# An adaLN attention block on one Trainium2 core: the opening of the kernel reordered (third x tile later, one copy on GpSimd, K rows and shift in another order)

## The chip, the core and the metric

The kernel runs on one core of a Trainium2 chip. Five engines work in it side by side, each through its own instruction queue in order: TensorE (PE in the profile; PEld is its weight load), VectorE (DVE), ScalarE (ACT), GpSimd (POOL) and SyncE (SP), which here only issues transfers from HBM to the on-chip memory (SBUF) and back. TensorE writes into the accumulation memory (PSUM), which VectorE and ScalarE read. The metric is the device time of one execution in microseconds (us), lower is better.

## What is computed

Inputs are bfloat16: x (2, 256, 1152), c (2, 1152), wqkv (1152, 3456), wo (1152, 1152), w_mod (1152, 6912).

```python
mod = (silu(c) @ w_mod).reshape(B, 6, 1, D)
shift_a, scale_a, gate_a, ... = mod[:, 0], mod[:, 1], mod[:, 2], ...
h = layernorm(x) * (1 + scale_a) + shift_a
q, k, v = split(h @ wqkv)                      # no bias, one head of width D
p = softmax(einsum("bqd,bkd->bqk", q, k) * D ** -0.5)
a = einsum("bqk,bkd->bqd", p, v) @ wo
out = x + gate_a * a                           # shift_m, scale_m, gate_m are not used
```

## The kernel before

**Tiles.** The 512 tokens are four tiles t = 0 to 3 of 128 (tiles 0 and 1 are batch 0, tiles 2 and 3 batch 1); the width D = 1152 is nine blocks k of 128. Everything is fed to TensorE with features on the partitions, so x is centred, turned by TensorE (`turned`, tiles `tp…`), and kept as `xnT[k, token]`.

**The order is written out.** The wrappers `vec`, `sca`, `ten`, `spq`, `gps` record every instruction, and `pin` (line 91) makes each engine run its list in the order of the program text. An engine that waits therefore holds up everything behind it. Because all instructions pass through the wrapper, the profile gives them all line 78; they are told apart by the names of their tiles.

**The opening (to about 31 us).** While the weights stream in, K is computed ahead of Q and V, in an unusual way: scale and centring are applied at once, `hTs = xnT * (1 + scale)`; the 1/sigma of a key is left for the softmax (a factor on the scores, from `rstd_bc`), and what shift adds to K is the same for every key, so softmax drops it. K needs `hTs` only. Q and V need `hT = xnT * rstd * (1 + scale) + shift`, hence the shift.

- *Transfers* (lines 151 to 174, in this order on SP): x tiles 1, 0, 3; the first three blocks of the scale weights `wS` in five pieces (`PAIRS`); K weights `wK` row 0 in two pieces, row 1; x tile 2; row 2; then scale weights and K rows in turns, the shift weights `wH`, the rest.
- *Fillers* (line 185): 13 products of no use, which keep TensorE running until data is there.
- *silu(c)*: VectorE makes `scT_f` (line 191); a ScalarE copy, `silu_rep` (line 201), repeats it 27 times into `scT_rep`, the moving operand of the scale products.
- *Scale, first part* (`scale_A`, line 307): 27 products into `psS0` and `psSA`, four rows of them behind the turned tile 1, five behind the turned tile 0.
- *Means*: tile 1 from VectorE's statistics, tiles 0 and 3 by ScalarE (`act_mean`, two instructions), tile 2 half by ScalarE and half by VectorE. `centre` (VectorE) writes `xc`.
- *K*: six accumulators `accs` (NACC = 6 blocks of 128 output features) take `k_part` (one block k, some of the tokens) as `hTs` becomes ready, later `k_step` (one block k, all 512 tokens). Output blocks 6 and 7 are held in two halves: k = 0 to 2 in `psE`/`early` (`early_half`), and k = 3 to 8 "parked" in `parked` (`k_block`). Output block 8 is `last_k`, nine products.
- *Scale, second and third part*: `psM` (blocks 3 to 5) and `psL` (blocks 6 to 8), each 27 products, then VectorE's `scaled_part`: one add and six `scaled` (one per block and batch).
- *Variance*: `dve_stats` (VectorE), `act_var` (ScalarE), then a GpSimd chain `rstd_parts`, TensorE's `rstd_turn` and `rstd_spread`, ScalarE's copy to `rstd_bc`, and nine VectorE products `xnT *= rstd_bc`.
- *Shift* (`shift_rows`, 36 products into `psH`), VectorE's block transpose to `sh`, then 18 instructions `modulated` that make `hT`: piece i is block i // 2 of batch i % 2; where i % 3 == 2 ScalarE makes it, else VectorE.

In the text of the program, the order around the shift is: `k_step(8)`; parked 6 and 7 (12 products); `psH`; the nine products of `last_k`; then Q, whose first product needs both pieces of `hT[0]`.

**The rest.** Q (81 products of 512 columns), scores `s_ps`, V, attention times V, the output product; VectorE sums the gate (`gacc`) meanwhile and GpSimd adds it over the partitions (`gate_bc`). PSUM: six buffers "mm", one "pa", one "pb"; a tile waits until its buffer's last reader is done.

Of the kernel before, what the change touches and what calls it, by code (L numbers as in the profile page):

```python
# [7 lines left out]
ACT = mybir.ActivationFunctionType  # L8
# [8 lines left out]
def kernel(  # L17
# [82 lines left out]
    def tok(b):  # L100
        return slice(b * N, (b + 1) * N)
# [40 lines left out]
    def load_x(t):  # L142
        spq.dma_start(out=x_sb[:, t, :], in_=x_f[t * P : (t + 1) * P, :])

    def load_mod(tile_, which, k0, k1, c0, c1):
        spq.dma_start(out=tile_[:, k0:k1, c0:c1], in_=wmod_v[:, k0:k1, which, c0:c1])

    def load_k(k0, k1, c0=0, c1=D):
        spq.dma_start(out=wK[:, k0:k1, c0:c1], in_=wqkv_v[:, k0:k1, D + c0 : D + c1])
# [2 lines left out]
    CA = KA * P  # L152
    load_x(1)
    load_x(0)
    load_x(3)
    for k0, k1 in PAIRS:
        load_mod(wS, 1, k0, k1, 0, CA)
    load_k(0, 1, 0, CA)
    load_k(0, 1, CA, WE)
    load_k(1, 2, 0, WE)  # L160
# [19 lines left out]
    def fillers(n):  # L180
        for _ in range(n):
            ten.matmul(junk_ps, lhsT=junk_rhs, rhs=junk_rhs.unsqueeze(1).to_broadcast([P, 4, P]),
                       start=True, stop=True)

    fillers(13)
    e_sb = small.tile([P, 2 * KT], F32, tag="e_sb")
    sca.activation(out=e_sb, in_=cT, func=ACT.Exp, scale=-1.0)
    scT_f = const.tile([P, KT, B], F32)
# [10 lines left out]
        )  # L199

    def silu_rep():
        sca.copy(out=scT_rep, in_=scT_f.unsqueeze(2).to_broadcast([P, KT, NR // B, B]))

    def sc_rhs(kk):
        return scT_rep[:, kk].rearrange("p r b -> p (r b)")
# [18 lines left out]
    def var_eps(t):  # L224
        gps.tensor_scalar(out=rstd[:, t : t + 1], in0=mv[:, t, 1:2], scalar1=1.0, scalar2=EPS,
                                op0=ALU.mult, op1=ALU.add)

    def act_mean(t):
        sca.activation(out=xc[:, t, :], in_=x_sb[:, t, :], func=ACT.Copy, accum_out=sums[:, t, 0:1])
        sca.activation(out=mv[:, t, 0:1], in_=sums[:, t, 0:1], func=ACT.Copy, scale=1.0 / D)  # L230

    HALF = D // 2
    half_sum = const.tile([P, 1], F32)

    def act_half_mean(t):
        sca.activation(out=xc[:, t, 0:HALF], in_=x_sb[:, t, 0:HALF], func=ACT.Copy, accum_out=sums[:, t, 0:1])

    def dve_half_mean(t):
        vec.reduce_sum(out=half_sum, in_=x_sb[:, t, HALF:], axis=AX.X)
        vec.tensor_scalar(out=mv[:, t, 0:1], in0=half_sum, scalar1=sums[:, t, 0:1], scalar2=1.0 / D,  # L240
                          op0=ALU.add, op1=ALU.mult)

    def act_var(t):
        sca.activation(out=square, in_=xc[:, t, :], func=ACT.Square, accum_out=sums[:, t, 1:2])
        gps.tensor_scalar(out=rstd[:, t : t + 1], in0=sums[:, t, 1:2], scalar1=1.0 / D, scalar2=EPS,
                                op0=ALU.mult, op1=ALU.add)
# [5 lines left out]
    def turned(tp, cols):  # L252
        for j, (t, k) in enumerate(cols):
            ten.transpose(tp[:, j, :], xc[:, t, k * P : (k + 1) * P], ident)

    def tiles_of(t, k0, k1):
        return [(t, k) for k in range(k0, k1)]

    def from_psum(eng, t, k0, k1, tp, j0=0):
        dst, srct = xnT[:, k0:k1, t * P : (t + 1) * P], tp[:, j0 : j0 + k1 - k0, :]  # L260
        if eng is vec:
            vec.tensor_copy(out=dst, in_=srct)
        else:
            sca.copy(out=dst, in_=srct)
# [22 lines left out]
    def rstd_spread():  # L287
# [9 lines left out]
    qkT = act.tile([P, 2 * KT, T], BF16)  # L297
    early = const.tile([P, NEARLY, T], F32)

    psSA = psum_a.tile([P, KA - 1, NR], F32, tag="pa")  # L300
    ten.matmul(psSA.rearrange("p j r -> p (j r)"), lhsT=ones_bf[0:1, :],
               rhs=ones_row[0:1, 0 : (KA - 1) * NR], start=True, stop=False, skip_group_check=True)
    psS0 = psum_b.tile([P, NR], F32, tag="pb")
    ten.matmul(psS0, lhsT=ones_bf[0:1, :], rhs=ones_row[0:1, 0:NR], start=True, stop=False,
               skip_group_check=True)

    def scale_A(kk):
        for j in range(KA):
            ten.matmul(
                psS0 if j == 0 else psSA[:, j - 1, :], lhsT=wS[:, kk, j * P : (j + 1) * P], rhs=sc_rhs(kk),  # L310
                start=False, stop=(kk == KT - 1), skip_group_check=True,
            )

# [24 lines left out]
    def one(t):  # L338
        return slice(t * P, (t + 1) * P)

    def scaled(k, sl, scalar):
        vec.tensor_scalar(out=hTs[:, k, sl], in0=xnT[:, k, sl], scalar1=scalar, scalar2=None, op0=ALU.mult)
# [40 lines left out]
    act_mean(0)  # L383
    centre(0)
    silu_rep()
    act_mean(3)

    def bank(name="tp", n=KT - KA, pool=psum, tag="mm"):
        return pool.tile([P, n, P], BF16, tag=tag, name=name)

    tp1a, tp1b, tp0a, tp0b = bank(n=KA), bank(), bank(n=KA), bank()
    turned(tp1a, tiles_of(1, 0, KA))
    turned(tp1b, tiles_of(1, KA, KT))
    from_psum(vec, 1, 0, KA, tp1a)
    from_psum(vec, 1, KA, KT, tp1b)
    for kk in range(4):
        scale_A(kk)
    turned(tp0a, tiles_of(0, 0, KA))
    turned(tp0b, tiles_of(0, KA, KT))
    from_psum(vec, 0, 0, KA, tp0a)  # L400
    from_psum(sca, 0, KA, KT, tp0b)
    for kk in range(4, KT):
        scale_A(kk)
    act_var(0)

    accs = [psum.tile([P, T], F32, tag="mm", name="acc") for _ in range(NACC)]
    scaled(0, tok(0), psS0[:, 0:1])
    vec.tensor_copy(out=s1p[:, 1:KA, :], in_=psSA[:, :, 0:B])
    vec.tensor_copy(out=s1p[:, 0, :], in_=psS0[:, 0:B])
    scaled(1, tok(0), s1p[:, 1, 0:1])  # L410
    centre(3)
    for k in range(2, KA):
        scaled(k, tok(0), s1p[:, k, 0:1])
    dve_stats(3, 0)
    psE = psum_a.tile([P, NEARLY, N], F32, tag="pa")
    k_part(0, tok(0), first=True)
    early_half(0, 0, psE)
    tp3 = bank(n=KT - 1, pool=psum_b, tag="pb")
    turned(tp3, tiles_of(3, 0, KT - 1))
    from_psum(vec, 3, 0, KA, tp3)  # L420
    for k in range(KA):
        scaled(k, one(3), s1p[:, k, 1:2])
    from_psum(sca, 3, KA, KT - 1, tp3, KA)
    act_half_mean(2)
    dve_half_mean(2)
    centre(2)
    k_part(1, tok(0))
    early_half(1, 0, psE)
    for k in range(KA - 1):
        k_part(k, one(3))  # L430
    early_half(2, 0, psE)
    sca.copy(out=early[:, :, tok(0)], in_=psE)
    k_part(2, tok(0))
    dve_stats(3, 1)
    tp2 = bank(n=KT - 1, pool=psum_b, tag="pb")
    turned(tp2, tiles_of(2, 0, KT - 1))
    from_psum(vec, 2, 0, KA, tp2)
    for k in range(KA):
        scaled(k, one(2), s1p[:, k, 1:2])
    from_psum(sca, 2, KA, KT - 1, tp2, KA)  # L440
    act_var(2)
    dve_stats(3, 2)
    dve_aggr(3)
    var_eps(1)
    var_eps(3)
    rstd_parts()
    k_part(KA - 1, one(3))
    psM = psum_a.tile([P, KA, NR], F32, tag="pa")
    for kk in range(KM):
        scale_part(psM, KA, kk)  # L450
    k_part(0, one(2))
    for kk in range(KM, KT):
        scale_part(psM, KA, kk)
    scaled_part(psM, KA)
    for k in range(1, KA):
        k_part(k, one(2))
    psE = psum_b.tile([P, NEARLY, N], F32, tag="pb")
    for k in range(KA):
        early_half(k, 1, psE)
    sca.copy(out=early[:, :, tok(1)], in_=psE)  # L460

# [3 lines left out]
    from_psum(vec, 3, KT - 1, KT, tp8, 0)  # L467
    from_psum(vec, 2, KT - 1, KT, tp8, 1)
    k_step(KA + 1)
    k_step(KA + 2, 0, 2)  # L470
    psL = psum_b.tile([P, KA, NR], F32, tag="pb")
    for kk in range(KT):
        scale_part(psL, KM, kk)
    scaled_part(psL, KM)
    k_step(KA + 2, 2, NACC)
    rstd_turn()
    k_step(KM)
    rstd_spread()
    for k in range(KT):
        vec.tensor_tensor(out=xnT[:, k, :], in0=xnT[:, k, :], in1=rstd_bc, op=ALU.mult)  # L480
    for k in range(KM + 1, KT):
        k_step(k)
    for f in range(NACC):
        evac(1, qkT[:, KT + f, :], accs[f])
# [1 line left out]
    for i in range(NEARLY):  # L486
        pool, tag = (psum_b, "pb") if i == 0 else (psum, "mm")
        parked.append(pool.tile([P, T], F32, tag=tag, name="ps"))
        k_block(NACC + i, parked[i], KA)
    psH = psum_a.tile([P, KT, 32], F32, tag="pa")  # L490
    for kk in range(KT):
        shift_rows(kk)
    vec.transpose(out=sh.rearrange("p f r -> p (f r)"), in_=psH.rearrange("p f r -> p (f r)"))
    for f in range(NACC + NEARLY, KT):
        ps = psum.tile([P, T], F32, tag="mm")
        for i, k in enumerate((*range(KA, KT), *range(KA))):
            ten.matmul(
                ps, lhsT=wK[:, k, f * P : (f + 1) * P], rhs=hTs[:, k, :], start=(i == 0), stop=(i == KT - 1),
            )
    last_k = ps  # L500

    def modulated(i):
        k, b = divmod(i, B)
        if i % 3 == 2:
            sca.activation(
                out=hT[:, k, tok(b)], in_=xnT[:, k, tok(b)], func=ACT.Identity,
                bias=sh[:, k, b : b + 1], scale=s1p[:, k, b : b + 1],
            )
        else:
            vec.tensor_scalar(  # L510
                out=hT[:, k, tok(b)], in0=xnT[:, k, tok(b)],
                scalar1=s1p[:, k, b : b + 1], scalar2=sh[:, k, b : b + 1],
                op0=ALU.mult, op1=ALU.add,
            )
# [47 lines left out]
        s_tiles.append(s_ps)  # L562

    gacc = act.tile([P, B, D], F32, tag="a3")
    gate_bc = const.tile([P, B, D], F32)

    def gate_step(i):
        b, kt = divmod(i, KT)
# [172 lines left out]
```

## Time and profile before

| | us |
|---|---|
| runs | 96.22, 96.24, 96.75; median 96.24 |
| the profiled execution | 96.45, its span 94.6 |
| TensorE busy / VectorE / ScalarE / GpSimd | 90.0 / 71.8 / 33.0 / 21.6 |
| granted TensorE clock | 1.00 throughout |
| DMA, 2.4 us to 52 us | 16 DMA engines 90% busy or more, 360 to 413 GB/s |

| stretch, us | TensorE busy | VectorE busy | ScalarE busy |
|---|---|---|---|
| 6.0 to 9.0 | 2.57 of 3.00 | 2.65 | 2.70 |
| 9.0 to 16.3 | 7.00 of 7.30 | 6.55 | 4.97 |
| 16.3 to 25.2 | 8.90 of 8.90 | 4.39 | 2.04 |
| 25.2 to 31.1 | 5.90 of 5.90 | 5.58 | 3.45 |

How to read it: times of instructions are counted from the start of the span. A row of the timeline gives the start of a group of like instructions, how long the group took, the engine, what it writes and reads, how many there were, and in brackets how long the engine had stood idle before, and what ended that. A matmul's own duration has its way through the array in it (a 128-column one shows 0.22), so TensorE's pace is read from one group's start to the next one's start.

### The profile page before, as it was taken

The numbers are of one execution on the slowest core, as the hardware profiler recorded it, in microseconds if no ns is written. First come the engines' busy times: TensorE is split into PE (matmuls) and PEld (weight loads), VectorE is DVE, ScalarE is ACT, GpSimd is POOL, SyncE is SP. The second block draws the span as 40 slices with busy tenths as digits, with TensorE's granted clock in tenths as the row PEclk, the third lists the DMA queues.
The fourth block names the chain that finished last, engine by engine and source line by source line (L and its number), as shares of the span: only waits on it lengthen the run. The fifth ranks groups of instructions, "written<-read, shape, count | busy, mean of one in ns | idle before, by whom it ended". The sixth has DMA issues, their size and how long they took to land.

```text
span 94.6 us, 1738 instructions
## 1 busy us (share of the span) xinstructions
PE 90.0 (95%) x682; PEld 54.5 (58%) x682; DVE 71.8 (76%) x140; ACT 33.0 (35%) x67; POOL 21.6 (23%) x27
## 2 busy tenths in 40 slices
PE   5998989999999999999999999999999999999980
PEld 1347979464445444444469656566579656565760
DVE  0398979234998999999997999991039487999870
ACT  5198747202753934222420465232225400000020
POOL 6700001810000000000000000009999970015000
PEclk9999999999999999999999999999999999999999
DMA  2999999999999999999999602200000000303221
GB/s 48 310 360 391 371 402 367 404 413 412 378 367 403 380 410 400 372 371 367 383 409 410 254 7 56 61 2 0 0 0 0 0 0 7 125 0 125 84 112 54
DMA packets 19015, 21.31 MB, mean 225 GB/s; under 512 B 2752, under 2 KB 13632, under 8 KB 19008
## 3 DMA queue, kind: packets, MB, share of 16 engines
q1 hardware_dynamic: 18592, 21.16, 62.1%
q10 hardware_dynamic: 416, 0.05, 0.4%
q8 instruction: 5, 0.08, 0.3%
q14 instruction: 2, 0.02, 0.0%
HBM read 19.76 MB, written 1.18 MB: 222 GB/s over the span
## 4 chain that ended last, share of the span: by engine, by line
PE 87%; DVE 4%; DMA 3%; ACT 2%; issue 1%
PE ps L78 65%; PE acc L78 11%; PE s_ps L78 4%; DMA x_sb<-in_x_dram 3%; PE tp L78 2%; DVE stats L78 2%; PE psH L78 1%; DVE xc L78 1%; PE psE L78 1%; PE psL L78 1%; ACT xnT L78 1%; PE psM L78 1%; ACT xc L78 1%; DVE mv L78 0%; PE psSA L78 0%
## 5 line engine op out<-in xcount | busy, mean ns | idle before, releaser
L78 POOL PARTITION_ALL_REDUCE gate_bc<-gacc x2 | 13.7, 6886 | 44.5 <-DVE gacc L78 44.5
L78 DVE SCALAR_TENSOR_TENSOR gacc<-wG,scT_f,gacc 128x1152 f32<-128x1152 bf16 x16 | 22.7, 1418 | 0.5
L78 PE MATMUL ps<-wqv,hT 128*128 128x384 bf16 x108 | 17.7, 326 | 0.0
L78 PE MATMUL ps<-hT,wqv 128*128 128x512 bf16 x81 | 17.6, 379 | 0.0
L78 PE MATMUL ps<-wO,attnT 128*128 128x384 bf16 (+1 forms) x108 | 17.0, 319 | 0.0
L78 PEld LDWEIGHTS <-attnT 128*128 128x128 bf16 x126 | 11.4, 98 | 6.3
L78 PEld LDWEIGHTS <-hT 128*128 128x128 bf16 x108 | 10.6, 98 | 6.9
L78 PEld LDWEIGHTS <-wK 128*128 128x128 bf16 x123 | 10.3, 97 | 6.7 <-issue 0.7
L78 PE MATMUL acc<-hTs,wK 128*128 128x128 bf16 (+2 forms) x90 | 13.5, 293 | 0.3 <-DVE hTs L78 0.3
L78 PEld LDWEIGHTS <-wqv 128*128 128x128 bf16 x81 | 7.9, 98 | 9.5
L78 ACT CAST qkT<-ps 128x512 bf16<-128x512 f32 x10 | 5.7, 584 | 10.8 <-PE ps L78 10.8
L78 DVE TENSOR_TENSOR ga<-ps,gate_bc 128x384 f32<-128x384 f32 (+1 forms) x12 | 6.5, 538 | 2.6 <-PE ps L78 2.6
L78 ACT CAST v_sb<-ps 128x384 bf16<-128x384 f32 x10 | 4.7, 476 | 9.8 <-PE ps L78 9.8
L78 DVE TENSOR_TENSOR o_sb<-ga,x_sb 128x384 bf16<-128x384 f32 (+1 forms) x12 | 6.8, 571 | 0.4
L78 DVE TENSOR_TENSOR xnT<-xnT,rstd_bc 128x512 bf16<-128x512 bf16 x9 | 5.5, 688 | 1.3 <-ACT rstd_bc L78 1.3
L78 ACT CAST o_sb<-ps 128x128 bf16<-128x128 f32 (+1 forms) x2 | 0.5, 238 | 17.0 <-PE ps L78 17.0
L78 PE MATMUL junk_ps<-junk_rhs 128*128 128x512 bf16 x13 | 5.3, 597 | 1.1 <-DVE junk_rhs L78 1.1
L78 DVE BATCH_NORM_STATS2 stats<-x_sb 128x6 f32<-128x384 bf16 x6 | 3.2, 554 | 2.7 <-DMA x_sb<-in_x_dram 2.7
L78 PE MATMUL ps<-hTs,wK 128*128 128x512 bf16 x21 | 4.9, 380 | 0.0
L78 DVE CAST attnT<-ps 128x512 bf16<-128x512 f32 (+1 forms) x6 | 3.5, 603 | 1.7 <-PE ps L78 1.7
L78 DVE CAST v_sb<-ps 128x384 bf16<-128x384 f32 x2 | 1.1, 558 | 4.6 <-PE ps L78 4.6
L78 DVE TENSOR_SCALAR hTs<-xnT,s1p 128x256 bf16<-128x256 bf16 (+1 forms) x20 | 4.3, 273 | 0.1
(85 smaller groups left out, 88.2 us busy)
## 6 DMA issues: line engine op xcount, KB each, us to landing
wqv<-in_wqkv_dram SPq DMA_DIRECT2D x5, 864.0 KB, 10.2
wG<-in_w_mod_dram SPq DMA_DIRECT2D x3, 864.0 KB, 9.5
wO<-in_wo_dram SPq DMA_DIRECT2D x3, 864.0 KB, 8.6
wH<-in_w_mod_dram SPq DMA_DIRECT2D x4, 576.0 KB, 8.3
wS<-in_w_mod_dram SPq DMA_DIRECT2D x6, 288.0 KB, 6.1
wK<-in_wqkv_dram SPq DMA_DIRECT2D x6, 288.0 KB, 6.3
x_sb<-in_x_dram SPq DMA_DIRECT2D x4, 288.0 KB, 3.5
wqv<-in_wqkv_dram SPq DMA_DIRECT2D x3, 288.0 KB, 8.4
```

The lines of the kernel that those rows point to most:

```text
L78: r = fn(*a, **k)
```

## The change

- *Transfers*: x tile 3 is loaded behind the five `wS` pieces, not ahead of them.
- *silu's copy* `scT_rep` is made by GpSimd, not by ScalarE. One filler fewer.
- *Means*: `act_mean` is one instruction (the scale 1/D is in it, its other output goes to `gate_bc`, which is not yet in use); tile 3 is now the one halved between ScalarE and VectorE, tile 2 goes to ScalarE alone.
- *Scale, first part*: one PSUM tile `psS`; four rows now run ahead of the turned tile 1, two ahead of the turned first half of tile 0, three behind it; one VectorE copy to `s1p`.
- *Copies from PSUM*: the second half of tile 1 goes to ScalarE.
- *K rows*: `k_part(1)` and its early half run ahead of the turned tile 3; the three rows of tile 3 behind row 2 of batch 0; `psM` runs in one piece ahead of tile 2's rows; two of VectorE's three statistics of tile 3 and `act_var(0)` come later; the early half of batch 1 runs behind `k_step(4)`, not ahead of `k_step(3)`.
- *Around psL and rstd*: three products (not four) follow `psL`; `rstd_turn` and `rstd_spread` sit inside the K rows 6 and 7.
- *Around the shift*: four of the nine products of `last_k` run ahead of `psH`. ScalarE makes the pieces with i % 3 == 1.

```diff
-    load_x(3)
     for k0, k1 in PAIRS:
         load_mod(wS, 1, k0, k1, 0, CA)
+    load_x(3)
...
-    fillers(13)
+    fillers(12)
...
-        sca.copy(out=scT_rep, in_=scT_f.unsqueeze(2).to_broadcast([P, KT, NR // B, B]))
+        gps.tensor_copy(out=scT_rep, in_=scT_f.unsqueeze(2).to_broadcast([P, KT, NR // B, B]))
...
-        sca.activation(out=xc[:, t, :], in_=x_sb[:, t, :], func=ACT.Copy, accum_out=sums[:, t, 0:1])
-        sca.activation(out=mv[:, t, 0:1], in_=sums[:, t, 0:1], func=ACT.Copy, scale=1.0 / D)
+        sca.activation(out=mean_junk, in_=x_sb[:, t, :], func=ACT.Copy, scale=1.0 / D, accum_out=mv[:, t, 0:1])
...
-    act_mean(3)
...
-    tp1a, tp1b, tp0a, tp0b = bank(n=KA), bank(), bank(n=KA), bank()
+    tp1a, tp1b, tp0a = bank(n=KA), bank(), bank(n=KA)
+    tp0b = bank(pool=psum_b, tag="pb")
+    for kk in range(4):
+        scale_A(kk)
     turned(tp1a, tiles_of(1, 0, KA))
     turned(tp1b, tiles_of(1, KA, KT))
     from_psum(vec, 1, 0, KA, tp1a)
-    from_psum(vec, 1, KA, KT, tp1b)
-    for kk in range(4):
+    from_psum(sca, 1, KA, KT, tp1b)
+    for kk in range(4, 6):
         scale_A(kk)
     turned(tp0a, tiles_of(0, 0, KA))
+    from_psum(vec, 0, 0, KA, tp0a)
+    for kk in range(6, KT):
+        scale_A(kk)
     turned(tp0b, tiles_of(0, KA, KT))
...
+    scaled(0, tok(0), psS[:, 0, 0:1])
+    vec.tensor_copy(out=s1p[:, 0:KA, :], in_=psS[:, :, 0:B])
+    scaled(1, tok(0), s1p[:, 1, 0:1])
+    act_half_mean(3)
     from_psum(sca, 0, KA, KT, tp0b)
-    for kk in range(4, KT):
-        scale_A(kk)
-    act_var(0)
...
+    dve_half_mean(3)
     centre(3)
     for k in range(2, KA):
         scaled(k, tok(0), s1p[:, k, 0:1])
-    dve_stats(3, 0)
     psE = psum_a.tile([P, NEARLY, N], F32, tag="pa")
     k_part(0, tok(0), first=True)
     early_half(0, 0, psE)
+    k_part(1, tok(0))
+    early_half(1, 0, psE)
+    act_mean(2)
     tp3 = bank(n=KT - 1, pool=psum_b, tag="pb")
     turned(tp3, tiles_of(3, 0, KT - 1))
...
-    act_half_mean(2)
-    dve_half_mean(2)
-    centre(2)
-    k_part(1, tok(0))
-    early_half(1, 0, psE)
-    for k in range(KA - 1):
-        k_part(k, one(3))
     early_half(2, 0, psE)
     sca.copy(out=early[:, :, tok(0)], in_=psE)
     k_part(2, tok(0))
-    dve_stats(3, 1)
+    centre(2)
+    dve_stats(3, 0)
+    for k in range(KA):
+        k_part(k, one(3))
...
+    act_var(0)
     act_var(2)
-    dve_stats(3, 2)
+    psM = psum_a.tile([P, KA, NR], F32, tag="pa")
+    for kk in range(KT):
+        scale_part(psM, KA, kk)
+    scaled_part(psM, KA)
+    for s in range(1, NCH):
+        dve_stats(3, s)
...
-    k_part(KA - 1, one(3))
-    psM = psum_a.tile([P, KA, NR], F32, tag="pa")
-    for kk in range(KM):
-        scale_part(psM, KA, kk)
-    k_part(0, one(2))
-    for kk in range(KM, KT):
-        scale_part(psM, KA, kk)
-    scaled_part(psM, KA)
-    for k in range(1, KA):
+    for k in range(KA):
         k_part(k, one(2))
-    psE = psum_b.tile([P, NEARLY, N], F32, tag="pb")
-    for k in range(KA):
-        early_half(k, 1, psE)
-    sca.copy(out=early[:, :, tok(1)], in_=psE)
...
     k_step(KA + 1)
-    k_step(KA + 2, 0, 2)
+    psE = psum_a.tile([P, NEARLY, N], F32, tag="pa")
+    for k in range(KA):
+        early_half(k, 1, psE)
+    sca.copy(out=early[:, :, tok(1)], in_=psE)
+    k_step(KA + 2, 0, 3)
     psL = psum_b.tile([P, KA, NR], F32, tag="pb")
     for kk in range(KT):
         scale_part(psL, KM, kk)
     scaled_part(psL, KM)
-    k_step(KA + 2, 2, NACC)
+    k_step(KA + 2, 3, NACC)
+    k_step(KM, 0, 3)
     rstd_turn()
-    k_step(KM)
+    k_step(KM, 3, NACC)
+    k_step(KM + 1, 0, 2)
     rstd_spread()
...
-    for k in range(KM + 1, KT):
+    k_step(KM + 1, 2, NACC)
+    for k in range(KM + 2, KT):
         k_step(k)
...
+    last_rows = (*range(KA, KT), *range(KA))
+    NFIRST = 4
...
+    last_block(0, NFIRST)
     psH = psum_a.tile([P, KT, 32], F32, tag="pa")
     for kk in range(KT):
         shift_rows(kk)
     vec.transpose(out=sh.rearrange("p f r -> p (f r)"), in_=psH.rearrange("p f r -> p (f r)"))
-    for f in range(NACC + NEARLY, KT):
-        ps = psum.tile([P, T], F32, tag="mm")
-        for i, k in enumerate((*range(KA, KT), *range(KA))):
-            ten.matmul(
-                ps, lhsT=wK[:, k, f * P : (f + 1) * P], rhs=hTs[:, k, :], start=(i == 0), stop=(i == KT - 1),
-            )
-    last_k = ps
+    last_block(NFIRST, KT)
...
-        if i % 3 == 2:
+        if i % 3 == 1:
```

`last_block(i0, i1)` is new: products i0 to i1 of the nine of `last_k`, in the order `last_rows`.

More of the change, by code (lines that the diff above doesn't have):

```diff
@@ L226, in var_eps @@
                                 op0=ALU.mult, op1=ALU.add)
+    gate_bc = const.tile([P, B, D], F32)
+    mean_junk = gate_bc[:, 0, :]
     def act_mean(t):
-        sca.activation(out=xc[:, t, :], in_=x_sb[:, t, :], func=ACT.Copy, accum_out=sums[:, t, 0:1])
-        sca.activation(out=mv[:, t, 0:1], in_=sums[:, t, 0:1], func=ACT.Copy, scale=1.0 / D)
+        sca.activation(out=mean_junk, in_=x_sb[:, t, :], func=ACT.Copy, scale=1.0 / D, accum_out=mv[:, t, 0:1])
     HALF = D // 2
@@ L235, in act_half_mean @@
     def act_half_mean(t):
-        sca.activation(out=xc[:, t, 0:HALF], in_=x_sb[:, t, 0:HALF], func=ACT.Copy, accum_out=sums[:, t, 0:1])
+        sca.activation(out=mean_junk[:, 0:HALF], in_=x_sb[:, t, 0:HALF], func=ACT.Copy, scale=1.0 / D,
+                       accum_out=sums[:, t, 0:1])
     def dve_half_mean(t):
         vec.reduce_sum(out=half_sum, in_=x_sb[:, t, HALF:], axis=AX.X)
-        vec.tensor_scalar(out=mv[:, t, 0:1], in0=half_sum, scalar1=sums[:, t, 0:1], scalar2=1.0 / D,
-                          op0=ALU.add, op1=ALU.mult)
+        vec.tensor_scalar(out=mv[:, t, 0:1], in0=half_sum, scalar1=1.0 / D, scalar2=sums[:, t, 0:1],
+                          op0=ALU.mult, op1=ALU.add)
     def act_var(t):
@@ L298 @@
     early = const.tile([P, NEARLY, T], F32)
[L300 to L305, printed above, removed]
+    psS = psum_a.tile([P, KA, NR], F32, tag="pa")
+    ten.matmul(psS.rearrange("p j r -> p (j r)"), lhsT=ones_bf[0:1, :],
+               rhs=ones_row[0:1, 0 : KA * NR], start=True, stop=False, skip_group_check=True)
     def scale_A(kk):
@@ L309, in scale_A @@
             ten.matmul(
-                psS0 if j == 0 else psSA[:, j - 1, :], lhsT=wS[:, kk, j * P : (j + 1) * P], rhs=sc_rhs(kk),
+                psS[:, j, :], lhsT=wS[:, kk, j * P : (j + 1) * P], rhs=sc_rhs(kk),
                 start=False, stop=(kk == KT - 1), skip_group_check=True,
@@ L394 @@
     from_psum(vec, 1, 0, KA, tp1a)
-    from_psum(vec, 1, KA, KT, tp1b)
-    for kk in range(4):
+    from_psum(sca, 1, KA, KT, tp1b)
+    for kk in range(4, 6):
         scale_A(kk)
     turned(tp0a, tiles_of(0, 0, KA))
+    from_psum(vec, 0, 0, KA, tp0a)
+    for kk in range(6, KT):
+        scale_A(kk)
     turned(tp0b, tiles_of(0, KA, KT))
-    from_psum(vec, 0, 0, KA, tp0a)
-    from_psum(sca, 0, KA, KT, tp0b)
-    for kk in range(4, KT):
-        scale_A(kk)
-    act_var(0)
[L406 to L410, printed above, removed]
+    accs = [psum.tile([P, T], F32, tag="mm", name="acc") for _ in range(NACC)]
+    scaled(0, tok(0), psS[:, 0, 0:1])
+    vec.tensor_copy(out=s1p[:, 0:KA, :], in_=psS[:, :, 0:B])
+    scaled(1, tok(0), s1p[:, 1, 0:1])
+    act_half_mean(3)
+    from_psum(sca, 0, KA, KT, tp0b)
+    dve_half_mean(3)
     centre(3)
@@ L489, with last_block @@
         k_block(NACC + i, parked[i], KA)
+    last_k = psum.tile([P, T], F32, tag="mm", name="ps")
+    last_rows = (*range(KA, KT), *range(KA))
+    NFIRST = 4
+    def last_block(i0, i1):
+        f = KT - 1
+        for i in range(i0, i1):
+            k = last_rows[i]
+            ten.matmul(
+                last_k, lhsT=wK[:, k, f * P : (f + 1) * P], rhs=hTs[:, k, :], start=(i == 0), stop=(i == KT - 1),
+                skip_group_check=True,
+            )
+    last_block(0, NFIRST)
     psH = psum_a.tile([P, KT, 32], F32, tag="pa")
@@ L564 @@
     gacc = act.tile([P, B, D], F32, tag="a3")
-    gate_bc = const.tile([P, B, D], F32)
     def gate_step(i):
```

## The prediction

> **What bounds the kernel now.** First the page: busy time by engine, then the chain by engine.
>
> ```profile
> PE 90.0 (95%) x682; PEld 54.5 (58%) x682; DVE 71.8 (76%) x140; ACT 33.0 (35%) x67; POOL 21.6 (23%) x27
> ...
> PE 87%; DVE 4%; DMA 3%; ACT 2%; issue 1%
> ```
>
> TensorE is 95% busy and 87% of the chain that ended last. The change leaves everything from Q on as it is, so the question is when Q's first product starts. Then the timeline of TensorE from 8.3 to 31.2 us, read from start to start:
>
> ```profile
> 8.89 0.81 PE L78 MATMUL acc<-hTs,wK 128*128 128x256 bf16 x6 [0.33 <-DVE hTs L78]
> ...
> 13.12 0.61 PE L78 MATMUL tp<-ident,xc 128*128 128x128 bf16 x8 [0.30 <-DVE xc L78]
> ...
> 19.48 0.85 PE L78 MATMUL psL<-scT_rep,wS 128*128 128x54 bf16 x27
> 20.18 1.02 PE L78 MATMUL acc<-hTs,wK 128*128 128x512 bf16 x4
> ...
> 25.21 2.75 PE L78 MATMUL ps<-hTs,wK 128*128 128x512 bf16 x12
> 27.89 1.29 PE L78 MATMUL psH<-wH,scT_rep 128*32 128x288 bf16 x36
> 29.11 2.12 PE L78 MATMUL ps<-hTs,wK 128*128 128x512 bf16 x9
> 31.06 0.38 PE L78 MATMUL ps<-hT,wqv 128*128 128x512 bf16 x1
> ```
>
> Two brackets mark idle time: before the first K product (VectorE's `hTs` ended it) and before the turned tile 2. Behind 16.3 us nothing waits. The timelines of VectorE and ScalarE from 29.0 us show what stands behind the shift:
>
> ```profile
> 29.23 0.48 DVE L78 STREAM_TRANSPOSE sh<-psH 128x288 f32<-128x288 f32 x1 [0.29 <-PE psH L78]
> 29.75 1.11 DVE L78 TENSOR_SCALAR hT<-xnT,s1p,sh 128x256 bf16<-128x256 bf16 x4
> 29.81 1.09 ACT L78 ACTIVATE hT<-xnT,sh,s1p 128x256 bf16<-128x256 bf16 x2 [2.45 <-DVE sh L78]
> ```
>
> `hT[0]` is ready near 30.35, Q starts at 31.06: 0.7 us of cover, from the nine `last_k` products (1.95 us).
>
> Paces, start to start: 54 columns 0.026 (psL, 27 in 0.70), a turn 0.056, 256 columns 0.109, 512 columns 0.216 (12 in 2.59). Lags: TensorE's end to VectorE 0.03, VectorE's end to TensorE 0.05.
>
> **Transfers.** Tile 3 is issued at 4.2, not 1.71, and lands near 7.9 (as many bytes ahead of it as ahead of the last `wS` piece: issued 4.19, 3.7 to landing). The `wS` pieces land some 0.9 earlier, what tile 3 took (4.56 to 5.5). SP waits for nothing new. All from `wK` row 0 on lands as now: 8.2 and 8.6 (issued 4.70, 5.18; 3.5 and 3.4 to landing), row 1 at 9.2 (5.65 + 3.6), tile 2 at 10.1 (6.13 + 4.0), row 2 at 10.7 (6.60 + 4.1).
>
> **The copy on GpSimd.** The trace has none. `scT_f` ends at 4.88, GpSimd is free from 4.25, so it starts near 4.97 (0.09 of lag, as between its own products). From below: ScalarE's copy of the same took 0.58. From above: `wo_last`, 192 elements of two inputs in 0.54, 2.8 ns each, so 486 x 2.8 = 1.37. The nearest GpSimd row by size with one input is the select on `pick` (512 elements, 0.64): I take 0.64 and an end at 5.6. TensorE wants it at 6.15, behind twelve fillers (the thirteenth started at 6.04) and the row of ones; the twelve products (0.31) end before the turned tile 1 can start at 6.69 (`xc` ends 6.63, unchanged). Cost 0 up to an end at 6.33. Queued behind a late copy are those twelve products, the turned tile 1 and all of K. At 1.37 the end is 6.34. The Trainium skill, page "SBUF — State Buffer", section "SBUF: two separate sides", speaks against this edit: a GpSimd instruction holds the port pair that it shares with VectorE for its whole length, and VectorE's double-port instructions wait. By that rule the sum is unchanged with an end at 5.6, and 0.23 us longer with an end at 6.34, as `centre(1)` (6.11) would wait. The nearest pair in the trace does not show it: beside GpSimd's one-element products (16.08 to 16.92) VectorE's six `hTs` products start every 0.2, as they do without them at 20.57.
>
> **First K product.** TensorE: tile 1 turned 6.69 to 7.19, two scale rows to 7.35, three turns to 7.51 (last ends 7.68, a turn lasting 0.22), three scale rows to 7.75, six turns to 8.08. VectorE copies the three turned blocks 7.71 to 8.06 (0.36; its copy of 768, 0.56, went to ScalarE: 0.80 at 7.39, ScalarE idle since 5.83), starts `hTs[0]` at 8.10, done 8.39; TensorE at 8.44. Now 8.89: **-0.45**.
>
> **Up to k_step(3).** k_part(0), (1) and their early halves end at 10.19 (row 1 lands 0.1 before its start at 9.31). VectorE: one copy, `hTs[1]`, half sum of tile 3 (0.75) 8.70 to 9.45, mean 9.69 (ScalarE's half ends 8.87), `centre(3)` 9.73 to 10.25; TensorE turns tile 3 at 10.30, idle 0.11. Early half 2 and row 2 end at 11.63, tile 3's rows (18 x 0.056) at 12.63. ScalarE takes tile 2's mean from 10.14 (landing) to 11.39; `centre(2)` stands behind tile 3's `hTs` on VectorE, 11.82 to 12.34: no idle time. Turned to 13.08, psM to 13.77; `hTs` of tile 2 at 13.91 (copy 13.26 to 13.62, product 0.26), idle 0.19. Its three rows end at 14.96. Idle 0.30 in all, now 0.59 (0.47 at 13.12, 0.10 at 14.46, 0.02 at 11.11): **-0.29**.
>
> `act_var(0)` moves behind tile 2's copy, so `act_var(2)` ends near 16.8, now 16.0. GpSimd's chain behind it (16.08 to 19.31, 3.23) ends near 20.1; `rstd_turn` comes at 21.2: hidden by 1.1. `act_mean(3)` and the short second instructions are off ScalarE: nothing, it had room.
>
> **Around psL.** k_step(3), two turns, k_step(4), early halves (0.66), three products: psL 18.97 to 19.66. `hTs[6]` for both batches ends 0.90 behind the start of psL's last product (now 20.15 to 21.06, VectorE's add and two `scaled`): 20.54. In between TensorE now has four products and the turn, 0.93, just enough; after, three, 0.65. A new wait: **+0.28**. It passes on to parked: 24.75 (now 25.21).
>
> **Around the shift.** Parked to 27.34, four of `last_k` to 28.21, 0.09 of switching as now: psH 28.30 to 29.52 (`wH`'s last piece lands 27.5). `psH` is thus 0.41 later than now, and `hT` with it. Piece 1 falls to ScalarE: 0.70 behind psH, 0.60 long, so `hT[0]` is ready at 30.82, Q at 30.87. The five products left end at 30.61: a second new wait, **+0.26**. VectorE is free for `sh` at 28.94 (nine products behind rstd_spread, 22.38, now 22.40). Later pieces come every 0.25 (VectorE) and 0.49 (ScalarE), under the 0.43 that two Q products take per block.
>
> **Sum.** -0.45 - 0.29 + 0.28 + 0.26 = -0.20; Q at 30.87. Behind it, VectorE starts the gate sums 0.4 later; it idles 0.6 before the first row maximum, so that is covered. `wqv`'s second and third chunks are wanted later than they land. The profiled execution took 96.45 (span 94.6, 1.85 around it), 0.21 over the median 96.24: 96.25 on its scale, **96.05** on the median's.
>
> **Rivals.**
> *The two new waits do not bind* (their sources are two VectorE lags, and a ScalarE start). Then -0.74, 95.5; if the 0.30 of idle time goes too, -1.04, 95.2. Against: the lag 0.90 and the pieces' lengths are read from this trace.
> *The weights come late.* K's rows 1 and 2 land 0.1 before use in my schedule, with the DMA engines full. If they come as late as the front is early, its 0.74 is lost and both waits stay: +0.54, 96.8. For: 382 GB/s from 6 to 16 us; against: no byte is moved ahead of them.
> *The copy on GpSimd is late.* In the trace, GpSimd's first `wo_last` product starts 7.17 us after the engine was done:
>
> ```profile
> 84.63 1.88 POOL L78 TENSOR_TENSOR wo_last<-wO,gate_bc 128x192 bf16<-128x192 bf16 x3 [7.17 <-issue]
> ```
>
> That is behind the reduction. Were the first copy to pay this, `scT_rep` would come at 12.8, 6.4 behind 6.33, and the time would be 102.5. The mechanism decides (slower than now) from an end at 6.53, a copy of 1.56; over 1% slower from 7.5, a copy of 2.5. Against: GpSimd's selects, memsets and small products start within 0.1 of the one before. The Trainium skill, page "GPSIMD Engine Reference", section "Instruction dispatch", has a kernel's first call after a load at about 6 us; with that figure the estimate would be 101.
>
> **Chances.** Under 1% (0.96 us) this kernel's runs, 0.5 apart, can hardly be told apart from no change. Forecast (95.6 to 96.5): 0.58, of it 0.02 beyond 1% on each side. No new waits: 0.18, of it 0.11 past 1%. Late weights: 0.14, of it 0.03 past 1%. Late copy: 0.10, of it 0.07 past 1%. Faster 0.02 + 0.11 = 0.13, slower 0.02 + 0.03 + 0.07 = 0.12, same 0.75. Range 95.2 (no waits at all) to 97.0 (late weights, with 0.2 for spread); outside are mostly the long copies.
>
> **What would show it.** In the changed profile: first K product near 8.44; tile 3 turned near 10.3; k_step(6) idle for some 0.3 on `hTs`; psH near 28.3, later than now though parked starts 0.45 earlier; Q near 30.9, waiting for ScalarE's `hT`. A GpSimd copy ending behind 6.3, or waits of TensorE on `wK`, would make it wrong upward; Q before 30.5 downward.

## The result, and the profile after

In ten runs each on one chip, the changed kernel took 97.44 us (median; 97.06 to 98.48), the kernel before 96.44 (96.22 to 97.14): a ratio of 1.0107, 95% interval 1.0068 to 1.0147. Repeated in a later session: 97.21, 1.0078 [1.0058, 1.0098]. It is about 1% slower; the forecast was 96.05, the range 95.2 to 97.0. The profiled execution of the changed kernel took 97.06 (span 95.2). It is the fastest of its ten, so its trace accounts for 0.6 of the 1.0 us lost; what the slower executions lost beyond that was not seen.

The page, busy time by engine and the chain by engine:

```profile
PE 89.9 (94%) x676; PEld 54.2 (57%) x680; DVE 71.2 (75%) x138; ACT 32.9 (35%) x65; POOL 22.3 (23%) x28
...
PE 82%; DMA 9%; DVE 2%; SPq 2%; ACT 1%; issue 1%; ACTq 0%
```

TensorE did the same work, 89.9 us, but its share of the chain fell from 87% to 82% and DMA's rose from 3% to 9%. The chain in order of time (start, length, what) says which transfer that is:

```profile
2.69 4.03 DMA wS<-in_w_mod_dram
6.71 0.02 issue
6.73 4.84 DMA wK<-in_wqkv_dram
11.57 0.05 issue
11.61 0.39 PE psE L78 x2
...
20.95 0.49 DVE hTs L78 x2
...
31.10 0.61 ACT hT L78
31.71 0.04 issue
31.75 10.09 PE ps L78 x46
```

Up to 11.6 us the chain runs through transfers and ends with `wK`'s row 2: its issue on SP waited for an earlier `wS` piece to land (6.73 instead of 6.60), it took 4.84 us from issue to landing instead of 4.1, and the early half that needs it is the next link. The two later links that are not TensorE's are the two new waits: `hTs[6]` behind psL, and ScalarE's `hT` behind the shift. TensorE's timeline (start, busy time, operation; idle time before it in brackets):

```profile
8.64 0.92 PE L78 MATMUL acc<-hTs,wK 128*128 128x256 bf16 x6 [0.32 <-DVE s1p L78]
...
9.91 0.83 PE L78 MATMUL acc<-hTs,wK 128*128 128x256 bf16 x6
...
10.80 0.61 PE L78 MATMUL tp<-ident,xc 128*128 128x128 bf16 x8
11.61 0.39 PE L78 MATMUL psE<-hTs,wK 128*128 128x256 bf16 x2 [0.21 <-DMA wK<-in_wqkv_dram]
...
13.50 0.61 PE L78 MATMUL tp<-ident,xc 128*128 128x128 bf16 x8
...
14.85 2.46 PE L78 MATMUL acc<-hTs,wK 128*128 128x128 bf16 x23
...
19.86 0.86 PE L78 MATMUL psL<-scT_rep,wS 128*128 128x54 bf16 x27
20.55 1.74 PE L78 MATMUL acc<-hTs,wK 128*128 128x512 bf16 x5
...
29.18 1.29 PE L78 MATMUL psH<-wH,scT_rep 128*32 128x288 bf16 x36
...
31.75 5.56 PE L78 MATMUL ps<-hT,wqv 128*128 128x512 bf16 x25
```

Against the forecast's stations: first K product 8.64 for 8.44; tile 3 turned 10.80 for 10.30; row 2 used 11.61 for 10.76; tile 2 turned 13.50 for 12.63; tile 2's rows 14.85 for 13.96; psH 29.18 for 28.30; Q 31.75 for 30.87. From row 2's use on, everything is 0.85 to 0.89 late, and that delay is all there when row 2 is used. Q stands 0.69 behind that of the kernel before (31.06).

### The profile page after: what moved, and what is told of

The parts are those of the page before. It is cut to its first block, busy times and chain, and to the rows that moved or that the text cites. A ratio compares the mean times of both kernels' runs of the same rounds, so it can differ in the third digit from the quotient of the medians.

```text
span 95.2 us, 1730 instructions
## 1 busy us (share of the span) xinstructions
PE 89.9 (94%) x676; PEld 54.2 (57%) x680; DVE 71.2 (75%) x138; ACT 32.9 (35%) x65; POOL 22.3 (23%) x28
## 4 chain that ended last, share of the span: by engine, by line
PE 82%; DMA 9%; DVE 2%; SPq 2%; ACT 1%; issue 1%; ACTq 0%
PE ps L78 63%; PE acc L78 11%; DMA wK<-in_wqkv_dram 5%; DMA wS<-in_w_mod_dram 4%; PE s_ps L78 4%; SPq L78 2%; PE psH L78 1%; PE psE L78 1%; DVE hTs L78 1%; PE psL L78 1%; ACT hT L78 1%; PE tp L78 1%; DVE sh L78 1%; DVE xnT L78 0%; PE spread_ps L78 0%
## 5 line engine op out<-in xcount | busy, mean ns | idle before, releaser
L78 PEld LDWEIGHTS <-attnT 128*128 128x128 bf16 x126 | 11.4, 98 | 6.3
L78 PE MATMUL junk_ps<-junk_rhs 128*128 128x512 bf16 x12 | 4.6, 567 | 1.1 <-DVE junk_rhs L78 1.1
## 6 DMA issues: line engine op xcount, KB each, us to landing
wqv<-in_wqkv_dram SPq DMA_DIRECT2D x5, 864.0 KB, 10.1
```

The lines of the kernel that those rows point to most:

```text
L78: r = fn(*a, **k)
```

## The experiments

Theory N: K's rows land when they land, about as late in any order; the forecast took one early profile for the rule, and only the changed order depends on the landing. Rival W: loading tile 3 behind the first part of scale made the rows late. Rival to both: the two new waits, or steps of the opening, cost more than forecast. All ratios are to the kernel before, run on the same chip.

| run | median us | ratio [95%] |
|---|---|---|
| e1, changed kernel again | 97.21 | 1.0078 [1.0058, 1.0098] |
| e2, tile 3 early again | 96.92 | 1.0075 [1.0045, 1.0106] |
| e3, before + tile 3 late | 97.97 | 1.0152 [1.0129, 1.0174] |
| e4, shift's wait undone | 96.88 | 1.0057 [1.0032, 1.0082] |
| e6, psL's wait undone | 97.11 | 1.0053 [1.0025, 1.0080] |
| e7, both undone | 96.81 | 1.0037 [1.0008, 1.0066] |
| e8, e7 + tile 2 behind row 2 | 96.89 | 1.0039 [1.0010, 1.0067] |
| e9, changed, 288 KB less | 96.96 | 1.0038 [1.0018, 1.0057] |
| e10, before, 288 KB less | 96.43 | 0.9987 [0.9973, 1.0001] |
| e11, e7, 288 KB less | 96.53 | 1.0005 [0.9978, 1.0032] |
| e12, e7 + tile 3 early | 96.58 | 1.0003 [0.9974, 1.0031] |
| e13, changed, 576 KB less | 96.55 | 0.9999 [0.9977, 1.0021] |
| e14, before, 576 KB less | 96.64 | 1.0018 [0.9998, 1.0038] |
| e15, e7, 576 KB less | 96.39 | 0.9993 [0.9970, 1.0016] |

**Is it tile 3's place? (e1, e2, e3)** e1 is the changed kernel; e2 puts one load back:

```diff
     load_x(0)
+    load_x(3)
     for k0, k1 in PAIRS:
         load_mod(wS, 1, k0, k1, 0, CA)
-    load_x(3)
```

> The changed kernel unaltered, for a second profile on the chip of the next three. Theory W (the weights come late because tile 3 now travels between the scale weights and the K rows): the K rows 1 and 2 land near 9.9 and 11.6 us again, TensorE waits for both, time 97.4. Rival V (the DMA stream merely varied in the one profile, and the time was lost elsewhere): rows back near 9.2 and 10.7, Q starts near 30.9, yet the time stays near 97.4.

> The changed kernel with tile 3 of x loaded ahead of the scale weights again; all else as changed. Theory W: rows 1 and 2 land near 9.2 and 10.7; the first four scale rows must now wait for their weights (6.6 us), which costs 0.2 at the first turns; TensorE waits for neither row; Q starts near 31.1, time 96.5 to 96.8. Rival C (the compute side, such as the copy on GpSimd or ScalarE's wider output, slows the stream): rows still at 9.9 and 11.6, time 97.2 or more.

e2 equals e1 in time, and its row 2 landed at 11.5 (issued 6.79, 4.7 us), as in e1 (6.61 + 4.8 = 11.4) and in the first profile (11.57). So W falls for the time and, as far as these profiles go, for row 2. For rows 0 and 1 it holds. These are the landings (us) in all profiles but e3's that have the same bytes ahead of the two rows:

| | row 0, first piece | row 1 | row 2 |
|---|---|---|---|
| tile 3 early (before, e5, e2, e12) | 8.2 to 8.4 | 9.2 to 9.6 | 10.7 to 11.9 |
| tile 3 late (changed, e1, e4, e6, e7, e8) | 8.6 to 9.1 | 9.9 to 10.5 | 11.4 to 11.8 (e8 moves it) |

Behind a late tile 3, rows 0 and 1 came about 0.6 and 0.7 later on average, and the two groups do not overlap; for row 2 they do. From 6 to 8 us the DMA engines moved 363 to 377 GB/s with tile 3 early and 285 to 346 with it late. Why the same bytes in this order travel more slowly is not shown.

e3 is the reverse edit on the kernel before, tile 3 moved behind scale's first part and nothing else:

> The kernel before with this one edit, tile 3 of x behind the scale weights. Theory W: rows 1 and 2 land at 9.6 us or later and 11.3 or later; the time grows by 0.3 to 0.6 besides, since ScalarE's mean of tile 3 starts 1.8 later and holds up a copy and centre(3). Rival C: rows at 9.2 and 10.7 as before, only the second part of the cost.

The rows came as W had it (row 1 at 10.3, row 2 at 11.7). At 1.0152 this is the slowest run of all, and the time grew by far more than the 0.3 to 0.6 expected. In the order of before, ScalarE takes tile 3's mean ahead of tile 0's copy, so a late tile 3 holds up that copy and what follows it. e3's profile (of its slowest execution, 99.39) shows it on ScalarE and on TensorE:

```profile
9.00 1.16 ACT L78 ACTIVATE xc<-x_sb 128x1152 bf16<-128x1152 bf16 x1 [2.48 <-DMA x_sb<-in_x_dram]
...
11.23 0.37 PE L78 MATMUL acc<-hTs,wK 128*128 128x256 bf16 x1 [1.19 <-ACT xnT L78]
```

Behind that wait the granted clock of this profile read 0.50 from 12 to 14 us, so its later stretches are not used here. The change carries its own remedy: there that mean stands behind tile 1's copy, split between two engines.

**The kernel before once more (e5)**, with no edit, for one profile (96.35 us):

> The kernel before, unaltered, for a second profile. Theory N (the weights land when they land, the first profile of this kernel was an early one, and it uses them late enough not to mind): K rows 1 and 2 land near 9.6 to 10.0 and 11.2 to 11.6 us, TensorE waits for neither (it uses them at 10.2 and 11.8), time within 0.3 of 96.4. Theory K (something in the changed kernel's computing slows its transfers): 9.2 and 10.7 again.

```profile
11.08 0.83 PE L78 MATMUL acc<-hTs,wK 128*128 128x128 bf16 x12
11.91 0.39 PE L78 MATMUL psE<-hTs,wK 128*128 128x256 bf16 x2
...
15.66 0.82 PE L78 MATMUL psE<-hTs,wK 128*128 128x256 bf16 x6
16.32 1.46 PE L78 MATMUL acc<-hTs,wK 128*128 128x512 bf16 x5
...
19.45 0.85 PE L78 MATMUL psL<-scT_rep,wS 128*128 128x54 bf16 x27
```

In this kernel, unchanged, row 2 landed at 11.9 (issued 6.81, 5.1 us), 1.2 later than in its first profile. Yet K's row 3 started at 16.32 (first profile: 16.35) and Q at 31.03 (31.06). The twelve products on tile 3 at 11.08 need rows 0 and 1 only; they fill the time, and the centring of tile 2 sets when the next turn can start. Row 2's own six products start at 12.14 and end near 12.80 (6 x 0.109), the turn starts at 13.09: about 0.3 of cover is left, so by this estimate the old order loses nothing up to a landing near 12.1. The forecast's 10.7 was the earliest landing of row 2 in the nine profiles in which it stands in its place with all bytes ahead of it (10.7; then 11.2 to 11.9; e3's is left out). The windows show the rate (columns: window, its length in us, busy time of PE, PEld, DVE, ACT, POOL, granted clock, DMA share, GB/s). The kernel before, first profile, then e5, then the changed kernel:

```profile
9.00:10.00 1.00, 1.00 (x13) 0.87 (x12) 1.00 (x4) 1.00 (x3) 0.00 (x0) 1.00 1.02 390
10.00:11.00 1.00, 1.00 (x15) 0.92 (x13) 0.88 (x4) 0.36 (x3) 0.19 (x1) 1.00 1.08 370
```

```profile
9.00:10.00 1.00, 1.00 (x13) 0.87 (x12) 1.00 (x4) 1.00 (x2) 0.00 (x0) 1.00 0.99 324
10.00:11.00 1.00, 1.00 (x15) 0.92 (x13) 0.88 (x4) 0.37 (x3) 0.19 (x1) 1.00 0.96 316
```

```profile
9.00:10.00 1.00, 0.86 (x8) 0.50 (x7) 0.86 (x3) 0.81 (x3) 0.00 (x0) 1.00 1.02 350
10.00:11.00 1.00, 1.00 (x12) 0.91 (x13) 0.68 (x2) 0.06 (x1) 0.00 (x0) 1.00 0.90 319
```

The DMA engines count as 90% busy or more in all six, and move 316 to 390 GB/s in the same stretch of the stream.

**The two new waits (e4, e6, e7)**, undone singly and together in the changed kernel:

```diff
-    NFIRST = 4
+    NFIRST = 0
-        if i % 3 == 1:
+        if i % 3 == 2:
```

```diff
-    k_step(KA + 2, 0, 3)
+    k_step(KA + 2, 0, 2)
     psL = psum_b.tile([P, KA, NR], F32, tag="pb")
...
-    k_step(KA + 2, 3, NACC)
+    k_step(KA + 2, 2, NACC)
```

> The changed kernel with all nine products of last_k behind the shift and ScalarE on the pieces with i % 3 == 2, as before; transfers as changed. Theory S (moving four products ahead of the shift costs a wait of 0.26 at Q): 0.26 less than the changed kernel, Q 1.95 us behind the shift's end without a wait. Rival: the shift's weights land late too (28.7 us for the last piece in the profile of the changed kernel), so the shift waits for them in its early place and nothing is gained (0 to 0.1).

> The changed kernel with four products, not three, behind psL; all else as changed. If the wait for hTs[6] is on the path (0.28 in the profile of the changed kernel), 0.22 less than the changed kernel, near 97.0. If the late weights alone set the time, nothing.

> The changed kernel with both waits undone: four products behind psL, all of last_k behind the shift, ScalarE on i % 3 == 2. If the two waits add up: 0.3 (the shift's part, measured) + 0.22 less than the changed kernel, 96.6 to 96.75. The difference that is left to the kernel before (0.1 to 0.3) is then what the late weights take. If the waits do not add up, as the shift's weights become the limit: 96.9.

Against e1, e4 takes 0.0021 of the ratio away (0.20 us), e6 0.0025 (0.24), both 0.0041 (0.40); expected were 0.26, 0.22 (the wait of 0.28 less what the product moved behind psL fills) and about 0.5. Each alone is within its intervals; together they are just clear of them, and somewhat smaller than expected. The profiles show both: from the parked blocks to Q it is 5.86 us in e4 (25.57 to 31.43) and 6.11 in the changed kernel (25.64 to 31.75), and from the early half of batch 1 to rstd's turn 3.36 in e6 (18.53 to 21.89) and 3.58 in the changed kernel (18.55 to 22.13). They are not the whole loss: e7 is still slower than before.

**Row 2 ahead of tile 2 (e8)**: e7 with `load_x(2)` moved behind `load_k(2, 3, 0, WE)`.

> As the one before, and tile 2 of x loaded behind K row 2. Row 2 lands 0.7 earlier, tile 2 0.7 later. If row 2 is what TensorE waits for at 11.5 us: 0.15 to 0.2 less than the one before (tile 2's mean then ends near 12.7, its turns start where they do now). If row 1 and row 0 hold it up as well, no more than 0.1.

Nothing was gained over e7, as the second half of the expectation has it. Row 2 came at 10.9 (6.19 + 4.7), but rows 0 and 1 (8.97 and 10.15) held TensorE up to 11.53 as well, and tile 2 of x came at 11.6, so its turn moved to 13.59, no earlier than in the changed kernel (13.50). The same bytes in another order changed which transfer is late.

**Fewer bytes ahead of the rows (e9 to e11; e13 to e15).** In e9 (changed), e10 (before) and e11 (e7) `load_x(3)` stands behind all of the K and scale weights; e13, e14 and e15 move `load_x(2)` there too. The opening reads another tile in their stead:

```diff
+    SRC = {0: 0, 1: 1, 2: 0, 3: 1}
...
-        vec.bn_stats(out=stats[t][:, s, :], in_=x_sb[:, t, s * CW : (s + 1) * CW])
+        vec.bn_stats(out=stats[t][:, s, :], in_=x_sb[:, SRC[t], s * CW : (s + 1) * CW])
```

and likewise in the means and the centring (`2: 2` in the lighter three).

> The changed kernel with 288 KB taken out of the stream ahead of the K rows: tile 3 of x is loaded behind all of the shift weights, and the opening uses tile 1's data in its place (means, statistics, centring of tile 3 are left out; only the residual uses tile 3). All instructions and their order stay. Theory L (the weights' landing sets the changed kernel's opening): rows 1 and 2 land 0.7 earlier, near 9.3 and 10.8, TensorE hardly waits for them, K row 3 starts 0.5 to 0.8 earlier, time 96.5 to 96.7. Rival E (the engines' own order sets it): no more than 0.2 less than the changed kernel, 97.0 or more.

> The same 288 KB taken out of the kernel before, in the same way. Theory L: it uses the rows later than they land anyway, so its time stays within 0.2 of 96.45. If the stream sets its opening too, it gains as much as the changed kernel, 0.5 or more.

> The changed kernel with both new waits undone (four products behind psL, all of last_k behind the shift) and the same 288 KB taken out. Theory L with the two waits: the opening's 0.6 to 0.74 comes out whole, 95.8 to 96.1, under the kernel before by 0.4 to 0.6. If the forecast of the opening itself was wrong: 96.3 or more.

> The changed kernel with two tiles of x (576 KB) moved behind all the weights that are wanted early; the opening takes the means, the statistics and the centred rows of tile 3 from tile 1's data, and those of tile 2 from tile 0's, so these of tiles 2 and 3 are left out. Theory L (only the weights' landing failed): row 2 of K lands before 10.7, and the stations of TensorE come at the forecast's times: tile 3 turned near 10.3, third psE pair near 10.8, tile 2 turned near 12.6, K's row 3 near 14.9, Q near 30.9, both new waits still there; 96.2, ratio to the kernel before 0.997. Theory E (the opening's steps were mis-costed as well): the rows are early, and K's row 3 stays behind 15.4; 96.8 or more, ratio 1.004.

> The kernel before with the same two tiles of x moved back and replaced in the opening (means, statistics and centred rows of tiles 2 and 3 left out). Theory L: the order of before is paced by centring, not by row 2, so K's row 3 moves little: the centring of tile 2 no longer waits for its landing, 0.2 to 0.4 of its idle time can go; 96.0 to 96.4, ratio 0.996 to 1.000. Theory E: the rows mattered here too; 95.7 or less, ratio under 0.994.

> The changed kernel without both new waits (two products ahead of psL as before; last block not begun ahead of the shift), and with the same two tiles of x moved back and replaced in the opening (means, statistics and centred rows of tiles 2 and 3 left out). Theory L: Q near 30.3, the whole 0.74 of the opening comes out; 95.7, ratio 0.992. Theory E: 96.4 or more, ratio 1.000.

The ratios side by side:

| order | all bytes | 288 KB less | 576 KB less |
|---|---|---|---|
| before | 1 | 0.9987 | 1.0018 |
| changed | 1.0078 | 1.0038 | 0.9999 |
| changed, no new waits | 1.0037 | 1.0005 | 0.9993 |

The order of before does not care how many bytes stand ahead of the rows; the changed order gains 0.4 us with each tile taken away, 0.0079 in all. That is the dependence which theory N names. A tile that is taken away can also be averaged and centred earlier; in the changed kernel's profile that is not what TensorE waits for: its wait names row 2, and tile 2's turn (13.50) follows the 24 products of 11.84 without a gap (6 x 0.109 + 18 x 0.056 = 1.66).

The size fell short of theory L. e10 came as expected by it; e14 (96.64) lies above its 96.4, and further still from the rival's 95.7; e13 (96.55) lies half way between the two theories. But e9 (96.96; rival: 97.0 or more), e11 (96.53; 96.3 or more) and e15 (96.39; 96.4 or more) lie where the rival has them, by which the forecast of the opening's own steps was too low. Three reasons show in the profiles.

The first is that fewer bytes did not bring the rows proportionally earlier. With 288 KB less, row 2 came at 12.1, 11.5 and 11.1 (e9, e10, e11), no earlier as a group than with all bytes; with 576 KB less it came at 10.1 to 10.4. e9's profile is of its slowest execution (97.70; row 1 at 10.0). TensorE's timeline of e9:

```profile
8.46 0.71 PE L78 MATMUL acc<-hTs,wK 128*128 128x256 bf16 x5 [0.28 <-DVE hTs L78]
...
12.14 0.39 PE L78 MATMUL psE<-hTs,wK 128*128 128x256 bf16 x2 [0.60 <-DMA wK<-in_wqkv_dram]
```

and of e13, where row 1 landed at 9.7 and row 2 at 10.4, ahead of its use:

```profile
6.34 0.30 PE L78 MATMUL psS<-ones_row,ones_bf 1*128 1x162 bf16 x1
...
8.72 0.82 PE L78 MATMUL acc<-hTs,wK 128*128 128x256 bf16 x6 [0.28 <-DVE hTs L78]
...
10.66 0.62 PE L78 MATMUL tp<-ident,xc 128*128 128x128 bf16 x8
11.12 0.38 PE L78 MATMUL psE<-hTs,wK 128*128 128x256 bf16 x2
...
13.03 0.61 PE L78 MATMUL tp<-ident,xc 128*128 128x128 bf16 x8
...
14.37 2.46 PE L78 MATMUL acc<-hTs,wK 128*128 128x128 bf16 x23
```

The second is the front: something else than the rows can delay it. In e9 the first K product came at 8.46 (forecast 8.44). In e13 it came at 8.72 though row 0 was there (7.9): the fillers ended at 6.34, the twelve scale products stand behind them, and tile 1's turn came at 6.89 instead of 6.61 (e9).

The third is the steps behind it. With rows 1 and 2 in time, tile 2's rows stand 5.65 behind the first K product (e13: 14.37 - 8.72, and the same in e15; forecast 13.96 - 8.44 = 5.52); in the changed kernel 6.21 (14.85 - 8.64). So the steps between were off by 0.13, and the landing made the rest of that stretch. In all, psL stands at 19.05 in e15 and at 19.16 in e13 (19.38 less its third product's 0.22), against 19.42 to 19.48 in the kernel before (first profile, e5, e10): the opening gains 0.3 to 0.4 there of the 0.74 forecast.

The ratios gain less than these profiles. Q comes 0.61 earlier in e15 than in e14 (30.69 against 31.30), but the medians are only 0.25 apart: e15's profile fell on its fastest run (95.92) and e14's on its slowest (97.10). What the rows did in the other executions was not seen.

**A version that computes everything (e12)**: e7 with tile 3 early again, as in e2.

> A candidate: the changed kernel with tile 3 of x back ahead of the scale weights and both new waits undone; it computes the reference whole. With tile 3 early 96.92 was measured, and both waits together took 0.4: 96.4 to 96.6, level with the kernel before, as the rows still land near 9.5 and 11.5.

1.0003 [0.9974, 1.0031], eleven of its twelve runs from 95.98 to 97.34: level with the kernel before, as expected, and more scattered. No version here beats it.

## Why the prediction was wrong, point by point

- **The step that failed**: "All from `wK` row 0 on lands as now: 8.2 and 8.6 ..., row 1 at 9.2 ..., row 2 at 10.7". In the changed profile row 1 landed at 9.9 (5.64 + 4.2) and row 2 at 11.57; in e7 the first K product itself waited 0.78 for row 0 (8.95), in e1 0.55. The step failed in two ways. Rows 0 and 1 did not land as before because of the change: tile 3, expected near 7.9, landed at 8.3 to 8.8, and they came behind it. Row 2's 10.7 was read from one execution, the earliest of nine. In the schedule built on these landings rows 1 and 2 had 0.1 of room. Of the 0.85 at row 2's use, 0.20 was there at the first K product; row 1 added 0.30 by tile 3's turn (10.80), row 2 a further 0.35. "SP waits for nothing new" was off by the 0.13 of row 2's issue.
- **Opening, -0.45 and -0.29**: both came out too large even with the rows in time: 0.3 to 0.4 together in e13 and e15. The first K product at 8.44 was met once (e9); in the other eleven profiles of the changed order it came at 8.61 to 9.14. In four of them row 0 was waited for; in four (e2, e8, e11, e13) the fillers ended at 6.34 and tile 1's turn came at 6.89 to 7.06, not 6.69. With the rows late the gain turned into a loss: psL less its third product stands at 19.64 (19.86 - 0.22), 0.16 behind the 19.48 of before.
- **GpSimd's copy, cost 0**: right, forecast 4.97 to 5.6. It ended before `centre(1)` started (6.18), so whether VectorE would wait for it was not put to the test:

```profile
5.01 0.59 POOL L78 CAST scT_rep<-scT_f 128x486 bf16<-128x486 f32 x1 [0.76 <-DVE scT_f L78]
```

- **psL, +0.28**: right. The three products behind it end near 21.20 (20.55 + 3 x 0.216), the next starts when `hTs[6]` is ready, at 21.48 in the chain.
- **The shift, +0.26**: right. psH at 29.18 is the forecast plus 0.88, `hT[0]` on ScalarE follows (31.10 to 31.71), Q at 31.75. In the timed runs undoing both waits gave back about 0.40 of the 0.5 expected.
- **rstd's chain, hidden**: right; GpSimd's last product starts at 20.67, the turn at 22.13.
- **The rival that came true** was "the weights come late", with a chance of 0.14 and a price of +0.54. The case against it, "no byte is moved ahead of them", counted bytes; the same bytes landed later in the new order (rows 0 and 1), and at different times in any order (row 2). Q's +0.69 is about 0.16 for the opening and 0.54 for the waits; the price lacked the 0.16, as rows at 11.6 take more than the 0.74 away. Working back from the trace, tile 2's rows follow row 2's landing by 3.28 (14.85 - 11.57), and psL less its third product by 8.07, so the changed order breaks even with before's 19.48 at a landing of 11.4. Of the nine profiles one was before 11 us, one at 11.2, and seven between 11.4 and 11.9.

What stays open: why the transfers differ between executions and with tile 3's place; what the slower executions lost, as both profiles of the unedited changed kernel are of its fastest ones; and why e12 came out lower than e7 (0.0034, within the intervals) while the same edit made no difference between e1 and e2. The landings would fit a reading: row 2 came at 11.2 in e12, so the earlier rows 0 and 1 could count, and at 11.5 in e2, so they could not. It was not tested.

## What to carry to other kernels

Before an order is tightened around a transfer, take its landing from several executions: work that runs ahead of a transfer without needing it is cover, even where one profile shows no wait. Moving that cover elsewhere trades a fixed gain for one that depends on when the transfer lands. Nor is a count of the bytes ahead enough: with tile 3 moved behind smaller pieces, the rows after it came later with the same bytes ahead of them. Ask of every new order at what landing it breaks even with the old, and how often the profiles lie on each side of it.

## What was not expected of the hardware

- **The spread of a landing.** Row 2, 256 KB, took 4.1 to 5.2 us from issue to landing in the nine profiles with the same bytes ahead of it. The Trainium skill, page "DMA: Bandwidth & Descriptors", section "Latency and other measured facts", has the access latency of HBM at 0.2 us on average and 2 us at high load; a spread of 1.1 us fits that, but no run here shows where in the transfer it arises.
- **Fewer bytes, no higher rate.** With tile 3 taken out, the kernel before (e10) moved 247 GB/s from 7 to 8 us, where it had moved 385. SP issues one transfer each 0.47 to 0.5 us, and around 4 us its transfers are of 96 and 160 KB: 160 KB in 0.47 us is 350 GB/s, 96 KB 210. That the issues limit the rate there is a reading, not tested by itself. (The rate of the kernel before was 310 GB/s from 2.4 to 4.7 us; 360 to 413 is what the later slices up to 52 us show.)
- **The fillers' end.** The fillers start at 1.10 or 1.11 in every profile. One takes 0.43 us at first and 0.22 later; the pace changes at the eighth in e9, and in e13 not before the last. So the product behind them comes at 5.35 in e9 and at 6.34 in e13; tile 1's turn, behind twelve scale products in the changed order, comes at 6.61 and 6.89. The granted clock reads 1.00 in all of these windows. The Trainium skill, page "TensorE: Matmul & The Clock Gate", section "Part 1: The HAM clock gate (the "warmup" mystery)", has the clock doubled after a free-running window of about 3.4 us, so that the moment depends on where the window stands, and 0.427 us as the slow pace for 512 columns; the two paces and ends 1 us apart agree with it.
